# Tap loads three apart, even phases turned first, a longer warm-up: one change to the start of a tuned convolution-and-joint kernel

## The chip, the cores and the metric

The kernel runs on one core of a Trainium2 chip. The metric is the device time of one execution in microseconds (us), the median of several. A second number that this text uses a lot is the span of the profiled execution; the time is 1.8 us longer than the span.

## The reference, cut to what matters

```python
B, T, D, K, U = 2, 4000, 512, 5, 8
xp = pad(x)                                  # x: (B, T, D) in bf16
h = sum(xp[:, i:i+T] @ w1[i] for i in 0..4)  # five taps; w1 is (5, 512, 512)
h = gelu(h)[:, ::2]
f = sum(hp[:, i:i+T1] @ w2[i] for i in 0..4)
f = gelu(f)[:, ::2]
j = tanh((f @ w_f)[:, :, None] + (g @ w_g)[:, None])
out = j @ w_o                                # (2, 1000, 8, 512)
```

## The kernel before

Time steps are kept as four phases (row 4n, 4n+1, 4n+2, 4n+3), with channels on the partitions. The convolution is computed from seven products ("a0", "b1", "b3", "a3", "b2", "a1", "a2") of sums and differences of phases, except for one piece: in the first tile, output column blocks 0 and 1 are computed tap by tap ("direct"), because that needs no sums of taps and can start as soon as one tap is there. "xf" makes a sum or difference on VectorE, "shift" a copy by one column on ScalarE. A small planner derives all waits between engines from the buffers that each operation reads and writes; loads are all issued by SyncE, in program order.

The first 256 columns of each phase of x come raw (`xr`, two loads of 512 KB) and are turned by TensorE; the rest comes by transposing DMAs (`load_x`).

```python
NWARM = 8
# ... cut
memset(zero[:])                                   # on GpSimd
# ... cut
act(warm[0:1], warm[1:2], ACT.Gelu_apprx_tanh)
xr_in = [load_xr(rt) for rt in range(2)]

def load_w1(i, after=None):
    o = load_w("sp", w1_sb[i], w1[i].rearrange("(k c) d -> c k d", c=P))
    if after is not None:
        o.deps[("dma", after.idx)] = True         # SyncE waits until that load has landed

load_w1(0)
for i in (1, 3, 4, 2):
    load_w1(i, xr_in[1])
for ph in (2, 3, 1, 0):
    load_x(0, ph, 272, 528)                       # transposing loads, second part of tile 0/1
# ... cut: load_x for two more segments

warm_mm(NWARM)
for rt in range(2):                               # half of the rows
    for pp in range(2):                           # even phases (0), odd phases (1)
        # ... cut: eight transposes on TensorE into bank 4 + 2 * pp + rt
        # even: copy to xs[0] on VectorE; odd: copy on ScalarE
    warm_mm(1 + rt)
# ... cut
for w in ("a0", "b1", "a3"):
    t0.shift(w)
for w in ("a1", "a2", "b3", "a0", "b1", "a3"):
    t0.xf(w)
wsum13(w1_sb, w1_t, "dve")
w1sums(1, "s")
for i in (0, 1, 3):
    direct(i)                                     # 16 matmuls of 254 columns each
filt("a0", "b1")                                  # a0 uses tap 0's weights, b1 tap 1's
direct(4)
filt("b3", "a3")
direct(2)
# ... cut
for w in ("a0", "b1", "a3"):
    t1.shift(w)                                   # ScalarE: wait for transposing loads
# ... cut: VectorE's sums
filt("b2", "a1", "a2")
for m in (0, 1):
    t0.gelu(m, ps.pair(m * NT, 256, NA))          # ScalarE: frees banks 0 and 1 for tile 1
```

## Time and profile before

| | before |
|---|---|
| time, median of the first 3 executions (lowest to highest) | 280.64 us (280.13 to 281.23) |
| span of the profiled execution | 278.82 us |
| first and second raw x load landed | 4.03, 5.28 us |
| taps 0, 1, 3, 4, 2 landed | 7.62, 10.74, 12.41, 13.81, 15.31 us |
| the four transposing loads of tile 1 landed | 16.16, 18.55, 19.30, 21.02 us |
| tap 0's matmuls start | 8.31 us |
| tile 1's first matmul (246 columns) | 23.81 us |

The landing times are those of the last of the sixteen marks that each load leaves on its semaphore in the trace. The Trainium skill, "DMA: Bandwidth & Descriptors", section "Why a DMA increments its semaphore by 16 and not by 1", says that a load is split over up to sixteen DMA engines which finish independently, and that only the full sixteen mean that all has landed.

The page of before, span, busy times, and the chain that ended last:

```profile
span 278.8 us, 3866 instructions
...
PE 273.8 (98%) x1435; PEld 138.8 (50%) x1435; DVE 188.1 (67%) x243; ACT 163.2 (59%) x193; POOL 30.9 (11%) x39
...
PE 95%; DMA 3%; issue 0%; DVE 0%; SPq 0%; DVEq 0%
```

The same chain in order of time (start, length, what it was):

```profile
1.17 4.11 DMA xr_64<-in_x_dram
...
5.30 5.44 DMA w_sb<-in_w_dram
...
10.78 264.00 PE acc L298 x1368
```

From 10.78 us TensorE works without a pause for 264 us. Nothing that the change touches lies inside that stretch but its first 13 us, so the change can win at the two ends only. The stretch begins when a tap load lands.

TensorE's timeline at the start (start, length, engine, line, operation, operands, count; in brackets the idle time before and what ended it):

```profile
4.68 1.91 PE L365 MATMUL acc<-ident,xr_63 128*128 128x128 bf16 x16
...
6.82 1.11 PE L365 MATMUL acc<-ident,xr_64 128*128 128x128 bf16 x16
...
8.31 1.90 PE L298 MATMUL acc<-xs_49,w_sb 128*128 128x254 bf16 x16
10.78 3.65 PE L298 MATMUL acc<-xs_49,w_sb 128*128 128x254 bf16 x32 [0.57 <-DMA w_sb<-in_w_dram]
...
23.81 0.37 PE L298 MATMUL acc<-xt_54,w_sb 128*128 128x246 bf16 x2
```

The two groups of sixteen transposes are the turning; the second, at a faster clock, takes 1.11 us where the first took 1.91. Tap 0's sixteen matmuls begin at 8.31, and the next ones wait for tap 1. The last line is tile 1's first matmul; its place measures how far ahead or behind TensorE is once the start is over.

ScalarE just before that, the copy "a3" of tile 1 and the two GELUs of tile 0:

```profile
21.04 1.02 ACT L291 ACTIVATE xt_54<-xs_49 128x984 bf16<-128x984 bf16 x1 [1.44 <-DMA xs_49<-in_x_dram]
21.97 1.06 ACT L291 ACTIVATE hT_61<-acc 128x508 bf16<-128x508 f32 x2
```

The copy waits for the fourth transposing load (landed 21.02); the GELUs stand behind it. They read the banks that tile 1's first matmuls write.

And the end, VectorE's last casts and SyncE's last two issues:

```profile
275.42 0.75 DVE L704 CAST ost_85<-acc 128x256 bf16<-128x256 f32 x2
...
275.90 0.93 SPq L712 DMA_DIRECT2D out_dram<-ost_85  x2
```

### The profile page before, as it was taken

How to read it: one execution, taken by the hardware profiler on the slowest of the kernel's cores; microseconds unless marked ns; L12 is line 12 of the kernel's file. 1: busy time of each engine (PE TensorE's matmuls, PEld its weight loads, DVE VectorE, ACT ScalarE, POOL GpSimd, SP SyncE). 2: the span in 40 equal slices, each digit the busy share in tenths (PEclk: the TensorE clock that was granted, in tenths of full speed). 3: DMA queues.
4: the chain of work that ended last, by engine and by line, in shares of the span. 5: the costliest groups of instructions: out<-in, count | busy, mean ns of one | idle time of the engine just before them, and what ended most of it. 6: DMA issues, size and time to landing. Idle time of an engine off the chain costs nothing.

```text
span 278.8 us, 3866 instructions
## 1 busy us (share of the span) xinstructions
PE 273.8 (98%) x1435; PEld 138.8 (50%) x1435; DVE 188.1 (67%) x243; ACT 163.2 (59%) x193; POOL 30.9 (11%) x39
## 2 busy tenths in 40 slices
PE   8999999999999999999999999999999999999995
PEld 4799954444444444444444444444444444444442
DVE  0899979866997676685434364776665766766764
ACT  2659738338327633822346475948957957966930
POOL 1000000079995000000000000000000000000000
PEclk9999999999999999999999999999999999999999
DMA  6999999992000000000000020444444445444444
GB/s 232 308 158 228 206 207 172 286 314 84 0 0 0 2 0 0 0 2 0 0 2 0 1 75 21 151 151 153 153 153 160 149 145 168 144 153 155 145 150 139
DMA packets 54719, 31.85 MB, mean 114 GB/s; under 512 B 31646, under 2 KB 54446, under 8 KB 54702
## 3 DMA queue, kind: packets, MB, share of 16 engines
q1 hardware_dynamic: 54702, 31.62, 42.4%
q8 instruction: 11, 0.18, 0.3%
q14 instruction: 6, 0.05, 0.1%
HBM read 7.86 MB, written 16.38 MB: 87 GB/s over the span
## 4 chain that ended last, share of the span: by engine, by line
PE 95%; DMA 3%; issue 0%; DVE 0%; SPq 0%; DVEq 0%
PE acc L298 95%; DMA w_sb<-in_w_dram 2%; DMA xr_64<-in_x_dram 1%; DVE ost_85 L704 0%; SPq L321 0%; DVEq L238 0%; DVE ost_84 L704 0%
## 5 line engine op out<-in xcount | busy, mean ns | idle before, releaser
L298 PE MATMUL acc<-wo_sb,jT 128*128 128x512 bf16 (+1 forms) x504 | 108.3, 377 | 0.0
L298 PEld LDWEIGHTS acc<-wo_sb,jT 128*128 128x128 bf16 x504 | 49.3, 98 | 58.8
L298 PE MATMUL acc<-xt_55,w_sb 128*128 128x500 bf16 (+1 forms) x192 | 42.1, 357 | 0.0
L291 ACT ACTIVATE jT<-feT_79,geT 128x1000 bf16<-128x1000 f32 (+6 forms) x44 | 35.8, 889 | 0.0
L291 ACT ACTIVATE jT<-feT_78,geT 128x1000 bf16<-128x1000 f32 (+4 forms) x40 | 35.1, 948 | 0.0
L298 PE MATMUL acc<-xt_54,w_sb 128*128 128x500 bf16 (+1 forms) x160 | 33.2, 342 | 0.0
L298 PEld LDWEIGHTS acc<-xt_55,w_sb 128*128 128x128 bf16 x192 | 18.8, 98 | 18.2
L291 ACT ACTIVATE cs_65<-acc 128x500 f32<-128x500 f32 (+2 forms) x13 | 7.0, 539 | 32.2 <-PE acc L298 32.2
L298 PEld LDWEIGHTS acc<-xt_54,w_sb 128*128 128x128 bf16 x160 | 15.6, 98 | 13.1
L291 ACT ACTIVATE cs_66<-acc 128x500 f32<-128x500 f32 (+2 forms) x13 | 7.0, 537 | 22.5 <-PE acc L298 22.5
L298 PE MATMUL acc<-xs_49,w_sb 128*128 128x254 bf16 (+2 forms) x112 | 15.7, 286 | 0.6 <-DMA w_sb<-in_w_dram 0.6
L291 ACT ACTIVATE ost_92<-acc 128x512 bf16<-128x512 f32 x10 | 6.0, 597 | 16.4 <-PE acc L298 16.4
L704 DVE CAST ost_81<-acc 128x512 bf16<-128x512 f32 x11 | 7.6, 691 | 10.4 <-PE acc L298 10.4
L704 DVE CAST ost_87<-acc 128x512 bf16<-128x512 f32 x10 | 6.9, 692 | 10.3 <-PE acc L298 10.3
L298 PE MATMUL acc<-xs_49,w_t 128*128 128x246 bf16 (+2 forms) x72 | 13.8, 315 | 0.0
L287 DVE TENSOR_TENSOR ty_68<-ty_68,acc 128x1000 f32<-128x1000 f32 (+2 forms) x9 | 9.7, 1077 | 5.2 <-PE acc L298 5.2
L287 DVE TENSOR_TENSOR ty_67<-ty_67,acc 128x1000 f32<-128x1000 f32 (+2 forms) x9 | 9.7, 1077 | 5.1 <-PE acc L298 5.1
L298 PEld LDWEIGHTS acc<-xs_49,w_sb 128*128 128x128 bf16 x112 | 10.7, 97 | 4.1 <-DMA w_sb<-in_w_dram 0.8
L291 ACT ACTIVATE ost_86<-acc 128x512 bf16<-128x512 f32 x10 | 5.9, 593 | 11.4 <-PE acc L298 11.4
L287 DVE TENSOR_TENSOR ty_69<-ty_69,acc 128x1000 f32<-128x1000 f32 (+1 forms) x8 | 8.5, 1061 | 3.5 <-PE acc L298 3.3
L298 PE MATMUL acc<-xt_55,w_t 128*128 128x500 bf16 (+1 forms) x48 | 10.0, 340 | 0.0
L704 DVE CAST ost_85<-acc 128x512 bf16<-128x512 f32 (+1 forms) x12 | 7.7, 646 | 2.6 <-PE acc L298 2.6
(113 smaller groups left out, 368.4 us busy)
## 6 DMA issues: line engine op xcount, KB each, us to landing
w_sb<-in_w_dram SPq DMA_DIRECT2D x10, 512.0 KB, 6.7
out_dram<-ost_81 SPq DMA_DIRECT2D x11, 128.0 KB, 1.9
out_dram<-ost_83 SPq DMA_DIRECT2D x10, 128.0 KB, 1.9
out_dram<-ost_85 SPq DMA_DIRECT2D x10, 128.0 KB, 1.9
out_dram<-ost_89 SPq DMA_DIRECT2D x10, 128.0 KB, 1.9
out_dram<-ost_82 SPq DMA_DIRECT2D x9, 128.0 KB
out_dram<-ost_84 SPq DMA_DIRECT2D x9, 128.0 KB
out_dram<-ost_86 SPq DMA_DIRECT2D x9, 128.0 KB
```

Source lines behind the costliest of these rows:

```text
L287: pl.op(eng, lambda e: e.tensor_tensor(out=o.ap, in0=a.ap, in1=b.ap, op=op), (a, b), (o,))
L291: pl.op("act", lambda e: e.activation(o.ap, i.ap, func, scale=scale, bias=0.0 if bias is None else bias.ap), rd, (o,))
L298: ins = e.matmul(o.ap, lhsT=l.ap, rhs=r.ap, start=start and n == 0, stop=stop and n == len(pairs) - 1, skip_group_check=not check)
L704: pl.op("dve", lambda e, o=o, v=v: e.tensor_copy(out=o.ap, in_=v.ap), (v,), (o,))
```

## The change

The intent: let tap 1 be on its way earlier, so that TensorE does not wait for it; start tap 0 earlier, by turning the even phases (all it needs) first; put one product of tap 0's weights right behind tap 0, as work that needs no further load; keep TensorE's clock up by a longer unbroken warm-up that starts sooner; and split the last output row's two halves over two engines.

```diff
-    NWARM = 8
+    NWARM = 10
-        memset(zero[:])
+        zv = zero[:]
+        pl.op("dve", lambda e: e.memset(zv.ap, 0.0), (), (zv,))
...
+        came = [load_xr(rt) for rt in range(2)]
         act(warm[0:1], warm[1:2], ACT.Gelu_apprx_tanh)
-        xr_in = [load_xr(rt) for rt in range(2)]
...
-        load_w1(0)
+            return o
+        came.append(load_w1(0))
         for i in (1, 3, 4, 2):
-            load_w1(i, xr_in[1])
+            came.append(load_w1(i, came[-3]))
...
-        for rt in range(2):
-            for pp in range(2):
+        for pp in range(2):
+            for rt in range(2):
...
-            warm_mm(1 + rt)
...
-            if which == "b3" and keep:
+            if which == "a0" and keep:
+                tt("dve", o(0), src[2, :, off - 1:off - 1 + n], ph(2), sub)
+            elif which == "b3" and keep:
...
-        for w in ("a0", "b1", "a3"):
+        for w in ("b1", "a3"):
             t0.shift(w)
-        for w in ("a1", "a2", "b3", "a0", "b1", "a3"):
+        for w in ("a0", "a1", "a2", "b3", "b1", "a3"):
             t0.xf(w)
...
-        for i in (0, 1, 3):
-            direct(i)
-        filt("a0", "b1")
+        direct(0)
+        filt("a0")
+        direct(1)
+        direct(3)
+        filt("b1")
...
-                if jt % 6 == 5 and not last:
+                if h == 1 or jt % 6 == 5 and not last:
...
-                    pl.dma("sp", lambda e, ...
+                    pl.dma(("sp", "act")[h], lambda e, ...
```

More of the change, by code (lines that the diff above doesn't have):

```diff
@@ L711, in bass_standalone__seq2seq_rnn_t_joint__speech_kernel @@
                     dst = out[b, t:t + n, u, cl]
-                    pl.dma("sp", lambda e, src=src, dst=dst: e.dma_start(dst, src.ap), (src,), (), slot_sem[s])
+                    pl.dma(("sp", "act")[h], lambda e, src=src, dst=dst: e.dma_start(dst, src.ap), (src,), (), slot_sem[s])
                     lo += n
```

## The prediction

> **What bounds the kernel.** TensorE. The chain of waits has one unbroken piece of 264.0 us of matmuls, from 10.78 us to 274.78 us of a 278.8 us span, and the mean granted clock is 1.0. Everything the change touches lies before 24 us or after 274 us, so only the two ends can give anything.
>
> **The start, before (timeline and landing times).** The two raw x loads land at 4.03 and 5.28 us, tap 0 at 7.62. Tap 0's sixteen matmuls start at 8.28 (after VectorE's copy of the second half, 7.51 to 8.20), and take about 1.75 us; TensorE then sits 0.57 us until tap 1 lands at 10.74. Taps 1, 3, 4, 2 are all issued from 5.30 on, behind the second x load; only 202 GB/s move between 6 and 7 us, against 350 to 375 GB/s once several loads are queued. On their slowest engine the taps land 1.4 to 1.7 us apart (10.74, 12.41, 13.81, 15.31).
>
> **What the change does.**
> 1. Tap 1 goes out at about 4.05 instead of 5.30 and queues right behind tap 0. Estimate: 7.6 + 1.5 = 9.1 us, then 10.7, 12.2, 13.8. TensorE never waits for a tap again.
> 2. Even phases turned first: tap 0 needs only these. Warm-up: ten matmuls of 427 ns from about 0.95 us (zero is filled by VectorE; before, the first ran at 1.30) end near 5.2. Turns cost 107 ns each cold and 56 ns warm (both seen), the warm clock came at 6.92. Both even copies done near 7.0 to 7.8, tap 0 starts at 7.65 to 8.3. The Trainium skill, "TensorE: Matmul & The Clock Gate", Part 1, says that the window deciding this runs freely, so the instant varies; this trace shows one switch only.
> 3. a0 by one VectorE subtraction from an unaligned operand, no ScalarE copy. Two pages of the skill disagree: "VectorE: DVE Perf Modes", Mode 2x_1P, asks for 4-byte alignment; "Vector Engine (DVE) Microarchitecture Reference", 5.1, says that it makes no difference. Aligned it takes 0.68 us; I expect 0.7 to 1.1. Either way it is ready before tap 0 ends. Its 0.9 us of matmuls bridge the time until tap 1.
>
> Tap 0 then ends at about 9.6 instead of 10.78: 0.8 to 1.4 us gained for TensorE.
>
> **What may take it back.** The transposing x loads are issued after tap 2, which now waits for tap 1: first issue about 9.6 instead of 7.41. Before, the first of them was stuck in its issue for 4.97 us and its packets hung until 15.07, when tap 2 finished on the slowest engine; as tap 2 comes 1.5 us earlier, I expect no delay. It matters: the last of the four (landing 21.02) gates ScalarE's a3 shift (21.04), which stands ahead of the two GELUs (end 23.03) that free the banks of the next tile's first matmul at 23.81. Slack is only about 0.8 us, so I take 0.2 us off. A landing after 22 us would cancel the gain.
>
> **The tail.** The last half row goes to ScalarE and its own DMA issue. Before, its cast started at 275.75 and its issue at 276.38; now about 275.65 and 276.1: 0.25 us.
>
> **Sum.** 280.64 - 1.2 + 0.2 - 0.25 = 279.4 us. Range 278.5 to 280.4. Faster by over 2%: 0.01; within 2%: 0.98; slower: 0.01.
>
> **What would show it.** Tap 1 landed before 9.6; no TensorE idle between tap 0 and the end; next tile's matmuls (first 246-column ones) starting at 22.5 to 23.0; fourth transposing load landed at or before 21; last output issue near 276.1 less the shift; middle unchanged at about 264 us.
>
> **What would make it wrong.** Transposing loads 1.5 us or more later; tap 0 slowed by tap 1 beside it; a late warm clock.

## The result, and the profile after

| | before | after |
|---|---|---|
| time, median of 6 (lowest to highest) | 280.79 us (279.54 to 281.23) | 279.36 us (278.72 to 279.52) |
| span of the profiled execution | 278.82 us | 277.59 us |
| taps 0, 1, 3, 4, 2 landed | 7.62, 10.74, 12.41, 13.81, 15.31 | 7.89, 9.29, 10.64, 12.99, 14.51 |
| transposing loads of tile 1 landed | 16.16, 18.55, 19.30, 21.02 | 17.02, 17.79, 18.89, 20.46 |
| tap 0's matmuls start | 8.31 | 7.93 |
| tile 1's first matmul | 23.81 | 22.70 |

The ratio of after to before is 0.9952, with a 95% interval of 0.9929 to 0.9975. (A ratio is the mean time of one kernel's fast runs over that of the other's of the same rounds, so it is not quite the ratio of the medians.)

The page and the chain of after:

```profile
span 277.6 us, 3862 instructions
...
PE 272.9 (98%) x1434; PEld 138.1 (50%) x1434; DVE 188.0 (68%) x243; ACT 162.7 (59%) x193; POOL 30.5 (11%) x38
...
PE 96%; DMA 2%; SPq 0%; ACT 0%; issue 0%
```

```profile
1.63 6.25 DMA w_sb<-in_w_dram
...
7.93 266.62 PE acc L298 x1392
...
274.57 0.38 ACT ost L291
```

The unbroken stretch of matmuls now begins with tap 0, at 7.93, and no load interrupts it. TensorE's timeline:

```profile
5.41 2.08 PE L367 MATMUL acc<-ident,xr 128*128 128x128 bf16 x32
7.93 1.92 PE L298 MATMUL acc<-xs,w_sb 128*128 128x254 bf16 x16 [0.44 <-DMA w_sb<-in_w_dram]
9.68 1.03 PE L298 MATMUL acc<-xt,w_sb 128*128 128x254 bf16 x8
10.55 3.64 PE L298 MATMUL acc<-xs,w_sb 128*128 128x254 bf16 x32
...
22.70 1.00 PE L298 MATMUL acc<-xt,w_sb 128*128 128x246 bf16 x8
```

All 32 transposes are one group; tap 0 waits for its load; a0's eight matmuls stand behind it; tap 1's follow with no idle time. ScalarE before tile 1, and the end of the kernel:

```profile
20.48 1.02 ACT L291 ACTIVATE xt<-xs 128x984 bf16<-128x984 bf16 x1 [1.50 <-DMA xs<-in_x_dram]
21.41 1.07 ACT L291 ACTIVATE hT<-acc 128x508 bf16<-128x508 f32 x2
```

```profile
273.70 1.02 DVE L709 CAST ost<-acc 128x512 bf16<-128x512 f32 x2 [0.17 <-PE acc L298]
274.57 0.38 ACT L291 ACTIVATE ost<-acc 128x256 bf16<-128x256 f32 x1 [3.73 <-PE acc L298]
274.99 0.38 ACTq L717 DMA_DIRECT2D out_dram<-ost  x1
```

The account of this pair of executions closes: tile 1 starts 23.81 - 22.70 = 1.11 us earlier. Of these, 0.73 us are the wait for tap 1 (from tap 0's first matmul to tile 1 it took 15.50 us before, 14.77 after) and 0.38 us are tap 0's earlier start (8.31 to 7.93). From there to the start of the last matmul both take 251.56 us (275.37 - 23.81 and 274.26 - 22.70). From the last matmul's start to the end of the span it is 3.45 us before and 3.33 after, 0.12 us less. 1.11 + 0.12 = 1.23 us, which is the difference of the spans (278.82 - 277.59).

That is an account of one execution of each. The experiments ask whether it holds for others.

### The profile page after: what moved, and what is told of

Same layout as the page of the kernel before. It is cut to its first block, busy times and chain, and to the rows that moved or that the text cites. A ratio compares the mean times of both kernels' runs of the same rounds, so it can differ in the third digit from the quotient of the medians.

```text
span 277.6 us, 3862 instructions
## 1 busy us (share of the span) xinstructions
PE 272.9 (98%) x1434; PEld 138.1 (50%) x1434; DVE 188.0 (68%) x243; ACT 162.7 (59%) x193; POOL 30.5 (11%) x38
## 3 DMA queue, kind: packets, MB, share of 16 engines
HBM read 7.86 MB, written 16.38 MB: 87 GB/s over the span
## 4 chain that ended last, share of the span: by engine, by line
PE 96%; DMA 2%; SPq 0%; ACT 0%; issue 0%
PE acc L298 96%; DMA w_sb<-in_w_dram 2%; SPq L322 0%; ACT ost L291 0%
## 5 line engine op out<-in xcount | busy, mean ns | idle before, releaser
L709 DVE CAST ost<-acc 128x512 bf16<-128x512 f32 (+1 forms) x105 | 72.2, 689 | 35.6 <-PE acc L298 35.6
L298 PE MATMUL acc<-xt,w_sb 128*128 128x500 bf16 (+2 forms) x352 | 75.3, 350 | 0.0
L291 ACT ACTIVATE jT<-feT,geT 128x1000 bf16<-128x1000 f32 (+5 forms) x84 | 70.9, 918 | 0.0
L298 PEld LDWEIGHTS acc<-xt,w_sb 128*128 128x128 bf16 x352 | 34.4, 98 | 31.3
L520 DVE SCALAR_TENSOR_TENSOR ty<-acc,cs 128x500 f32<-128x500 f32 (+2 forms) x52 | 29.7, 613 | 23.8 <-PE acc L298 22.9
L287 DVE TENSOR_TENSOR ty<-ty,acc 128x1000 f32<-128x1000 f32 (+2 forms) x26 | 27.9, 1072 | 14.4 <-PE acc L298 13.6
L298 PE MATMUL acc<-xs,w_t 128*128 128x500 bf16 (+2 forms) x136 | 29.9, 342 | 0.0
L298 PE MATMUL acc<-xs,w_sb 128*128 128x254 bf16 (+2 forms) x144 | 23.8, 305 | 0.4 <-DMA w_sb<-in_w_dram 0.4
L291 ACT ACTIVATE xt<-xs 128x2000 bf16<-128x2000 bf16 (+2 forms) x14 | 21.5, 1568 | 3.7 <-DMA xs<-in_x_dram 3.7
L291 ACT ACTIVATE hT<-ty 128x1000 bf16<-128x1000 f32 (+2 forms) x18 | 17.4, 965 | 1.7 <-DVE ty L287 1.6
L298 PE MATMUL acc<-fT,wf_sb 128*128 128x500 bf16 x64 | 13.8, 374 | 0.0
```

The costliest lines, as they stand in the source:

```text
L287: pl.op(eng, lambda e: e.tensor_tensor(out=o.ap, in0=a.ap, in1=b.ap, op=op), (a, b), (o,))
L291: pl.op("act", lambda e: e.activation(o.ap, i.ap, func, scale=scale, bias=0.0 if bias is None else bias.ap), rd, (o,))
L298: ins = e.matmul(o.ap, lhsT=l.ap, rhs=r.ap, start=start and n == 0, stop=stop and n == len(pairs) - 1, skip_group_check=not check)
L520: pl.op("dve", lambda e, o=o, f=f: e.scalar_tensor_tensor(out=o.ap, in0=d.ap, scalar=f, in1=c.ap, op0=ALU.mult, op1=add), (d, c), (o,))
L709: pl.op("dve", lambda e, o=o, v=v: e.tensor_copy(out=o.ap, in_=v.ap), (v,), (o,))
```

## The experiments

The first four kernels (e1 to e4) ran on one chip, the other eight on another; there is no e5. Each has 5 rounds, except e6 and e7 with 3. "Before of the same rounds" is the kernel before, on the same chip.

My first theory (A) was that of the prediction: because tap 1 is issued at 5.30 behind the second x load, it lands near 10.7 in every execution, and TensorE waits. Rival B: it is the earlier start of tap 0 that counts.

### Pacing alone

Before, with only the tap loads' waits changed (run e1_pace):

```diff
-        xr_in = [load_xr(rt) for rt in range(2)]
+        came = [load_xr(rt) for rt in range(2)]
...
-            load_w1(i, xr_in[1])
+            came.append(load_w1(i, came[-3]))
```

> The kernel before with one thing changed: each tap load waits for the load three ahead of it (tap 1 goes out when the first x load has landed). Theory A (the idle time before tap 1 was the cost, and pacing removes it): tap 1 lands near 9.3 us instead of 10.74, tap 0's matmuls still start near 8.3 and end near 10.0, TensorE goes on without idling; the first 246-column matmul starts at 23.1 to 23.3 instead of 23.81; time 0.5 to 0.7 us below before. Rival B (the earlier start of tap 0 by even phases first is what counts): no more than 0.2 us gained.

Measured: tap 1 landed at 9.12, tap 0's matmuls started at 8.30. The timeline of TensorE in this run:

```profile
8.30 4.94 PE L298 MATMUL acc<-xs,w_sb 128*128 128x254 bf16 x44
...
23.05 1.00 PE L298 MATMUL acc<-xt,w_sb 128*128 128x246 bf16 x8
```

One group from tap 0 on: the idle time is gone, as theory A says, and tile 1 starts at 23.05, 0.76 us before the place in the profile of before. But the times say less: ratio 0.9989 (0.9974 to 1.0003), 0.3 us instead of 0.5 to 0.7, and not clear of noise. Before was itself faster in these rounds (median 279.67) than in the first comparison (280.79). Something in before varies.

### Everything but pacing and tail

After, with the old waits of the tap loads and the old tail (run e2_even):

```diff
-            came.append(load_w1(i, came[-3]))
+            came.append(load_w1(i, came[1]))
...
-                if h == 1 or jt % 6 == 5 and not last:
+                if jt % 6 == 5 and not last:
...
-                    pl.dma(("sp", "act")[h], lambda e, ...
+                    pl.dma("sp", lambda e, ...
```

> The kernel after with the old pacing (taps 1, 3, 4, 2 all wait for the second x load) and the old tail; even phases first, longer warm-up, a0 used behind tap 0 are kept. Theory A says that tap 1 still lands near 10.7, but tap 0 (about 7.8 to 9.6) and now also a0's 0.86 us of matmuls are done by then, so TensorE idles only from about 10.5 to 10.75: first 246-column matmul at 22.9 to 23.1, time 0.6 to 0.9 us below before. So pacing and bridging are two cures of one wait and do not add up. Rival B (pacing is needed for any gain): no more than 0.2 us below before.

Measured: tap 1 landed at 9.54, not near 10.7, although it was again issued behind the second x load. Tap 0 ran from 7.39, a0 from 9.14, tap 1 from 10.01, without idle time; tile 1 at 22.15. Ratio 0.9984 (0.9964 to 1.0005). The bridge worked as said: without a0's matmuls TensorE would have stood from 9.1 to 9.6. The landing contradicts theory A.

### After without the bridge

Run e3_nobridge:

```diff
-        direct(0)
-        filt("a0")
-        direct(1)
-        direct(3)
-        filt("b1")
+        for i in (0, 1, 3):
+            direct(i)
+        filt("a0", "b1")
```

> The kernel after with a0's matmuls put back behind taps 0, 1, 3. In the profile of after tap 1 had landed at 9.29, before tap 0's matmuls ended near 9.7, so theory A expects no difference to after beyond 0.2 us: first 246-column matmul at 22.6 to 22.9, time 1.0 to 1.4 us below before. Rival (the bridge is what covers the wait even with pacing): TensorE idles 0.3 us or more before tap 1's matmuls and the time is 0.3 us or more above after's.

Measured: tap 1 at 8.49; tap 0, 1 and 3 in one group from 7.50 (48 matmuls); tile 1 at 22.25; ratio 0.9984 (0.9969 to 0.9998). No idle time: with pacing, the bridge covers nothing in this execution. Tile 1 came a little earlier than I had said (22.6 to 22.9) because tap 0 started earlier than in the profile of after. The time was 0.4 us below before's, not the expected 1.0 to 1.4.

### Even phases first, without pacing, bridge and tail

The edits of the last two together (run e4_even_nobridge).

> The kernel after with the old pacing, the old tail and a0's matmuls put back behind taps 0, 1, 3: of the start only the even phases first and the longer warm-up remain. Theory A: tap 0's matmuls start at 7.7 to 8.0 but TensorE then idles about 1 us until tap 1 lands near 10.7; first 246-column matmul at 23.7 to 23.9 and time as before within 0.2 us. Rival B: 0.3 to 0.5 us gained, as much as tap 0 starts earlier.

```profile
7.86 5.38 PE L298 MATMUL acc<-xs,w_sb 128*128 128x254 bf16 x48
...
22.61 1.00 PE L298 MATMUL acc<-xt,w_sb 128*128 128x246 bf16 x8
```

Theory A failed: no idle time, since tap 1 landed at 9.33 and tap 0 only ended at 9.6. The ratio, 0.9996 (0.9981 to 1.0010), is "as before within 0.2 us", as theory A had said, but not for its reason. I looked at the sixteen marks of tap 1 again. In the profile of before, fourteen of them stand between 8.64 and 9.13, and two at 10.55 and 10.74. So 10.74 was two stragglers, and that is theory C. (They were not of tap 1 alone: taps 3 and 4 in the same profile also have two marks that come 1.2 us or more after the fourteenth, and tap 2 no longer.)

### Before and after again

The next four texts are those of before_again, after_again, before_third and after_third, which are the two kernels unchanged. A "look" is one profiled execution.

> The kernel before itself, a second look at its start, and a control of the noise: ratio 1.000 within 0.002. The four runs so far showed tap 1 landing at 9.3 to 9.5 us even with the old pacing, which speaks against my theory A. Theory A (with the old pacing tap 1 lands near 10.7 in every execution, because it is issued at 5.3): tap 1 at 10.5 to 10.9 again, and TensorE idle about 0.6 us before its matmuls. New theory C (10.74 was a straggler: fourteen of its sixteen parts were there by 9.13, and such stragglers come in some executions only): tap 1 at 9.1 to 9.6, tap 0's matmuls from 8.1 to 8.3, no idle time behind them, first 246-column matmul at 22.9 to 23.1.

> The kernel after itself beside before on the same chip. Theory A: ratio near 0.995 again. Theory C: what remains for certain is tap 0's earlier start (0.4 to 0.8 us) and the tail (0.14 us), so the ratio is 0.9965 to 0.9985 where before has no straggler, and larger gains come only from executions of before with one; first 246-column matmul at 22.2 to 22.8.

> The kernel before, a third look. Its executions so far fall in two groups, 279.2 to 279.7 and 280.5 to 281.2. Theory C says that the start of the next tile is tap 1's landing plus 13.1 us, so the profiled execution's first 246-column matmul is at 22.4 to 22.7 if its time is 279.2 to 279.6, and at 23.6 to 24.0 with tap 1 landing at 10.5 to 10.9 if its time is above 280.4. If a long execution shows tap 1 on time, theory C is wrong about the long group.

> The kernel after again, beside e8 and e9 on the same chip: ratio to before 0.995 to 0.998, first 246-column matmul at 22.2 to 22.8, no execution above 279.8 us.

TensorE's timeline of the second and of the third look at before:

```profile
7.10 1.90 PE L298 MATMUL acc<-xs,w_sb 128*128 128x254 bf16 x16
9.40 1.81 PE L298 MATMUL acc<-xs,w_sb 128*128 128x254 bf16 x15 [0.40 <-DMA w_sb<-in_w_dram]
```

```profile
7.39 1.90 PE L298 MATMUL acc<-xs,w_sb 128*128 128x254 bf16 x16
9.73 1.48 PE L298 MATMUL acc<-xs,w_sb 128*128 128x254 bf16 x12 [0.44 <-DMA w_sb<-in_w_dram]
```

Tap 1 landed at 9.35 and 9.69: no stragglers, as theory C says. But TensorE still waited for it, which theory C had not said for the second look: tap 0 had started early there, at 7.10 and 7.39 instead of 8.1 to 8.3, because the full clock came at 4.41 and 5.00 us (6.92 in the first). So the wait for tap 1 is in all three looks at before, and its end is tap 1's landing: tile 1 started 13.07 us after it each time (23.81 - 10.74, 22.42 - 9.35, 22.76 - 9.69). Part of what an early clock gives is lost in before to this wait.

The third look's time was 279.56 us, and tile 1 at 22.76 misses the 22.4 to 22.7 that I had put beside such a time by 0.06.

After's second and third look: tap 1 at 8.69 and 8.95, tap 0 from 7.80 and 7.20, tile 1 at 22.56 and 21.96 (the latter earlier than the 22.2 I had as a lower edge), ratios 0.9956 (0.9932 to 0.9980; a larger gain than the 0.9965 to 0.9985 of theory C, in rounds in which before had long executions) and 0.9981 (0.9962 to 1.0000; just outside the 0.995 to 0.998 that I had said). Before against itself gave 0.9978 (0.9952 to 1.0004; I had allowed 0.002) and 1.0016 (0.9993 to 1.0040). So a single ratio here is uncertain by some 0.2%, and the ratios of e1 to e4, 0.9984 to 0.9996, can't rank the parts of the change; only the traces can.

The looks so far in one table. "Full clock" is the instant from which the trace records the whole clock as granted, "first matmul" is tap 0's; the rule beside it is worked out below.

| run | full clock | tap 0 landed | first matmul | tap 1 landed | tile 1 | rule |
|---|---|---|---|---|---|---|
| before | 6.92 | 7.62 | 8.31 | 10.74 | 23.81 | tap 1 + 13.07 |
| before_again | 4.41 | 6.88 | 7.10 | 9.35 | 22.42 | tap 1 + 13.07 |
| before_third | 5.00 | 6.95 | 7.39 | 9.69 | 22.76 | tap 1 + 13.07 |
| e4_even_nobridge | 6.26 | 6.76 | 7.86 | 9.33 | 22.61 | first + 14.75 |
| e2_even | 4.51 | 7.34 | 7.39 | 9.54 | 22.15 | first + 14.76 |
| e1_pace | 6.89 | 7.74 | 8.30 | 9.12 | 23.05 | first + 14.75 |
| e3_nobridge | 5.51 | 7.06 | 7.50 | 8.49 | 22.25 | first + 14.75 |
| after | 5.67 | 7.89 | 7.93 | 9.29 | 22.70 | first + 14.77 |
| after_again | 6.14 | 7.29 | 7.80 | 8.69 | 22.56 | first + 14.76 |
| after_third | 4.62 | 7.15 | 7.20 | 8.95 | 21.96 | first + 14.76 |

Two chains run against each other. Without the bridge, tile 1 starts at the later of "first matmul + 14.76" and "tap 1 + 13.07". In before the second is the later one in three of three looks. Every kernel of the table that has pacing, or the bridge, is on the first rule. The one with neither, e4, is there by the luck of a late clock: its two sides were 22.62 and 22.40. In after's third look the second side would have been 8.95 + 13.07 = 22.02, so that there alone the bridge covered something with pacing, 0.06 us.

The times don't contradict this, but they don't show it either. Of the 51 executions of before in all these comparisons, 37 lie between 279.13 and 280.19 (mean 279.59) and 14 between 280.39 and 281.38 (mean 280.85). With only 0.2 us between them, the two groups are my division. The 42 executions of the kernels with pacing and unchanged transposing loads (after, e1, e3, and two below) have none over 279.84; that highest one is e1's, whose clock came as late (6.89) as in before's first look. The 12 of e2 and e4, without pacing, have three over 279.84. The highest, 280.33, is of e2, where the bridge would have hidden most of a wait for a tap 1 that landed at 10.74 (estimate: less a0's matmuls, 9.68 to 10.55 after, tile 1 is at 10.74 + 13.07 - 0.87 = 22.94, and the time 279.8). So something else can also lengthen an execution. The only profiled execution of before's upper group is the first one (280.62 us), with the two stragglers; I did not catch another. That all long executions have this cause is not shown.

### The transposing loads held back

The prediction named one way to lose the gain. After (run e6_late_x), with

```diff
-            load_x(0, ph, 272, 528)
+            load_x(0, ph, 272, 528).deps[("dma", came[-1].idx)] = True
```

(and `load_x` returning its load), so that the first transposing load waits for tap 2's landing, and the same with the GELUs ahead of the copy (run e7_late_x_gelu):

```diff
-        for w in ("a0", "b1", "a3"):
+        for w in ("a0", "b1"):
             t1.shift(w)
...
+        for m in (0, 1):
+            t0.gelu(m, ps.pair(m * NT, 256, NA))
+        t1.shift("a3")
         for w in ("a1", "a2", "a3"):
             t1.xf(w)
         filt("b2", "a1", "a2")
-        for m in (0, 1):
-            t0.gelu(m, ps.pair(m * NT, 256, NA))
```

> The kernel after, its first transposing x load held until tap 2 has landed (about 14.5 us instead of issuing at 9.7). Tests the prediction's one way to lose the gain: the fourth of these loads gates ScalarE's a3 copy, which stands ahead of the two GELUs that free the next tile's banks. Expected: fourth landing at 22.5 to 25, first 246-column matmul at that landing plus 2.2 us (24.7 to 27), TensorE idle before it by what it is late, time 2 to 4 us above after. Rival (the GELUs and banks have more slack than I read): start below landing plus 1.5 us.

> As e6_late_x, but with the two GELUs put ahead of ScalarE's a3 copy, so that they no longer wait for the fourth transposing load. If the order on ScalarE is the gate, the first 246-column matmul comes back to about 22.7 whatever the landing, and TensorE waits only later, for VectorE's a1 operand of that tile (landing plus 0.9 us or more, first wanted 1.7 us after the tile's start): 1 to 2.5 us of e6's loss come back. If the loads themselves are the gate (operands), nearly nothing comes back.

The timeline of the first, ScalarE and TensorE:

```profile
22.75 1.02 ACT L291 ACTIVATE xt<-xs 128x984 bf16<-128x984 bf16 x1 [1.99 <-DMA xs<-in_x_dram]
23.68 1.07 ACT L291 ACTIVATE hT<-acc 128x508 bf16<-128x508 f32 x2
...
24.32 1.01 PE L298 MATMUL acc<-xt,w_sb 128*128 128x246 bf16 x8 [1.37 <-ACT hT L291]
```

The fourth load landed at 22.73, the copy and the first GELU followed, and TensorE idled 1.37 us until the GELU was done. The gate is real. It is smaller than I had read: tile 1 starts 1.59 us after the landing, not 2.2, because the first matmuls need only the first GELU's bank (the first GELU ended at 24.27, the second at 24.75). The start is 1.54 us later than tap 0's start plus 14.76 would be. The median was 280.31 us (ratio 1.0005, 0.9975 to 1.0035), about 1.2 us above after, less than the 2 to 4 that I had expected.

The second:

```profile
20.14 1.07 ACT L291 ACTIVATE hT<-acc 128x508 bf16<-128x508 f32 x2
22.10 1.02 ACT L291 ACTIVATE xt<-xs 128x984 bf16<-128x984 bf16 x1 [0.89 <-DMA xs<-in_x_dram]
...
22.83 1.00 PE L298 MATMUL acc<-xt,w_sb 128*128 128x246 bf16 x8
```

With the GELUs first, tile 1 starts at 22.83 (first matmul 8.08 + 14.75) although the fourth load landed at 22.07. TensorE then waits only 0.2 us, before the matmuls at 25.56, for VectorE's a3 operand (I had named a1). Median 279.75 us, ratio 0.9978 (0.9945 to 1.0010): 0.6 us of e6's 1.2 came back in the median of four, where I had said 1 to 2.5, and 1.3 us in the profiled pair. So the order on ScalarE was the gate.

In after the gate's slack was 22.70 - (20.46 + 1.59) = 0.65 us. In after's third look it was nought: 20.38 + 1.59 = 21.97, and tile 1 started at 21.96.

### Eight warm-up matmuls, and eight with the GELUs first

Runs e8_warm8 and e9_warm8_gelu:

```diff
-    NWARM = 10
+    NWARM = 8
```

> The kernel after with eight warm-up matmuls instead of ten (that part of the change undone). In the profiles of after the ten end near 5.4 us, while the first x load has been there since 4.0; tap 0's start (7.8 to 7.93) follows the second even copy or tap 0's landing, whichever is later. If the longer warm-up only holds the turning back: turning from 4.55, second even copy done at 7.0 to 7.3, tap 0's matmuls at 7.1 to 7.5 unless tap 0 lands later, first 246-column matmul at 21.8 to 22.3, time 0.2 to 0.5 us below after. Rival (the longer warm-up pays, by an earlier full clock): the clock turns full later than with ten, and the time is after's or 0.2 us above it.

> e8_warm8 with the two GELUs ahead of ScalarE's a3 copy, as in e7_late_x_gelu. With the start pulled forward the gate seen in e6 (fourth transposing load plus 1.6 us) comes near: 20.0 to 20.5 plus 1.6 is 21.6 to 22.1. If it binds in e8, this run starts the next tile 0 to 0.3 us earlier than e8; if it doesn't, it equals e8. A version meant to beat both: ratio to before 0.993 to 0.997.

VectorE and TensorE in the run with eight, then in the run that also has the GELUs first; VectorE's first subtraction (a0) begins when both even copies are done:

```profile
6.90 1.28 DVE L287 TENSOR_TENSOR xt<-xs 128x1016 bf16<-128x1016 bf16 x2
...
8.01 1.15 PE L298 MATMUL acc<-xs,w_sb 128*128 128x254 bf16 x9 [0.98 <-DMA w_sb<-in_w_dram]
```

```profile
7.06 1.29 DVE L287 TENSOR_TENSOR xt<-xs 128x1016 bf16<-128x1016 bf16 x2
...
7.44 1.81 PE L298 MATMUL acc<-xs,w_sb 128*128 128x254 bf16 x15 [0.26 <-DMA w_sb<-in_w_dram]
```

With eight the even phases were ready at 6.90 and 7.06, at full-clock instants of 5.18 and 5.97. With ten they were ready at 7.00, 7.51 and 7.74, at 4.62, 5.67 and 6.14. On a straight line through the values with ten, the two extra matmuls hold the turning back by 0.4 us at a clock of 5.18 and by 0.6 us at 5.97, and the clock came no later with eight. But both profiled executions then waited for tap 0 itself (landed 7.97 and 7.40), so tile 1 started at 22.78 and 22.21, the first of them outside the expected 21.8 to 22.3. The times: medians 278.82 and 278.84, ratios 0.9968 (0.9949 to 0.9986) and 0.9975 (0.9955 to 0.9994), against 279.17 and 0.9981 for after in the same rounds. e9's ratio misses the 0.993 to 0.997 that I had said. Whether eight beats ten is not settled by 0.1% with such intervals; that the longer warm-up pays is not seen anywhere. Between e8 and e9 nothing was seen: in neither did the fourth transposing load bind (20.80 + 1.59 = 22.39 against 22.78, and e9 no longer depends on it).

The same reading, when both even copies are done, can be taken in before. The third looks at before and at after, VectorE's first sum or subtraction:

```profile
7.32 1.28 DVE L287 TENSOR_TENSOR xt<-xs 128x1016 bf16<-128x1016 bf16 x2
```

```profile
7.00 1.28 DVE L287 TENSOR_TENSOR xt<-xs 128x1016 bf16<-128x1016 bf16 x2
```

With the old order (before's three looks and e1) it began at 7.03, 7.32, 8.23 and 8.24, at full-clock instants of 4.41, 5.00, 6.89 and 6.92: a straight line within 0.01 us. Each of the six kernels with even phases first, ten warm-up matmuls and a recorded instant lies 0.13 to 0.14 us below that line, the two with eight 0.5 and 0.7 us below it. So what even phases first gains, the longer warm-up mostly takes back. And the start was then often held up elsewhere: in six of the ten looks with even phases first, after's first and third among them, TensorE idled 0.23 to 0.98 us until tap 0 had landed. The prediction had named tap 0 slowed by tap 1 beside it as a risk. In the nine looks with pacing tap 0 landed at 6.94 to 7.98 (mean 7.49), in the five without at 6.76 to 7.62 (mean 7.11); these overlap, so that pacing delays tap 0 is not shown.

## Why the prediction was right or wrong

The number was right: 279.4 predicted, 279.36 measured. Step by step:

- **Only the two ends can give anything.** Right. From tile 1's start to the last matmul it is 251.56 us in both.
- **The start gains 0.8 to 1.4 us, 1.2 taken.** In the pair of profiled executions it was 1.11. The mechanism, a wait for tap 1 that goes away, is right: it is in three of three looks at before and in none at after. What was wrong is that I took the 10.74 of one execution for the rule, when two of its sixteen parts were late. (The spacing of 1.4 to 1.7 us held: 1.51, 1.51 and 1.57 in the second look.) Without stragglers tap 1 lands at 9.35 to 9.7 in before, and the gain of the start is smaller: from the second and third looks, the mean of tile 1's start is 22.59 before and 22.26 after, 0.33 us (a rough figure, from two looks each at different clock instants). The first comparison's 0.48% rests on six executions of before, four of them in the upper group. Over all executions here the means are 279.93 (51 of before) and 279.12 (18 of after), 0.8 us or 0.3%.
- **Tap 0 starts at 7.65 to 8.3 by even phases first.** It started at 7.93, but mostly by luck. Of the 0.73 us by which the even phases were ready sooner (8.24 to 7.51), 0.6 are the earlier clock (6.92 to 5.67, along the line above) and 0.13 the change; then tap 0's late landing, 7.89, took 0.35 us back. No run shows that the change moves the clock: it came at 4.41 to 6.92 in the four looks with the old start, at 4.51 to 6.26 in the six with ten matmuls.
- **Tap 1 near 9.1, taps after it near 10.7, 12.2, 13.8.** Measured 9.29, 10.64, 12.99, 14.51. The first two are right, the last two landed 0.7 to 0.8 us later than said. Taps 4 and 2 were not waited for.
- **a0's matmuls bridge the time until tap 1.** They stand there, but with pacing there was almost nothing to bridge: in the profile of after tap 1 landed at 9.29 and tap 0's matmuls ended near 9.7, and moving a0 back changed nothing that could be seen (e3). Pacing and bridge are two cures of one wait.
- **The longer warm-up.** I costed it and did not ask what it holds back. Even phases were ready 0.4 and 0.6 us sooner with eight.
- **Alignment of a0.** The prediction left open 0.7 or 1.1 us. It is 0.69, as for an aligned operand (next section).
- **The transposing loads are not delayed, 0.2 us off for the gate.** The first landed 0.86 us later than before and the last 0.56 us earlier. The gate exists (e6, e7), but took nothing: I had counted both GELUs where the first is enough. This term was 0.2 and should have been 0.
- **The tail, 0.25 us.** The last issue came 0.28 us earlier relative to the last matmul (276.38 - 275.37 = 1.01 before, 274.99 - 274.26 = 0.73 after), but its data landed 1.89 us after the issue instead of 1.72, so 0.12 remained. In the looks, six with the old tail have 3.44 to 3.46 us from the last matmul's start to the end, and eight with the new one 3.31 to 3.34. This term was sized at twice its worth.

The two wrong sizes, 0.2 taken off needlessly and 0.13 too much at the tail, and a start of 1.11 for 1.2, nearly cancel: -1.2 + 0.2 - 0.25 = -1.25 against -1.11 - 0.12 = -1.23. The close agreement of the sum is partly luck, as is the 1.11 itself, from one execution of before with a late clock and stragglers and one of after with an earlier clock.

## What to carry to other kernels

When a profile shows an engine waiting for a load, look at how the parts of that load landed, and at a second execution, before taking the landing time for a constant; a gain that was read from one profile with a straggler (1.11 us here) need not be that of the next ones (0.33). Compare starts at the same instant of the full clock, or the clock's luck is taken for the change's gain. Two cures of one wait do not add up. Ask of each instruction that waits for a load what stands behind it on its engine: two GELUs behind a copy were a gate that came into reach as soon as the start moved forward, and moving them ahead took it away at no cost that could be seen (e8 and e9: 278.82 and 278.84 us).

## What the Trainium skill lacked or had wrong

- "VectorE: DVE Perf Modes", section "Mode 2×_1P — pack two bf16 into one 32-bit read", asks for 4-byte alignment. The a0 subtraction has one operand that starts one bf16 element off that grid and took 0.692 us; the aligned sum of the same 128x1016 shape that stood first in before took 0.686. "Vector Engine (DVE) Microarchitecture Reference", section 5.1, says that alignment makes no difference, and is right here. In the profile of after's second look:

```profile
7.74 0.69 DVE L287 TENSOR_TENSOR xt<-xs 128x1016 bf16<-128x1016 bf16 x1
```

- "TensorE: Matmul & The Clock Gate", Part 1, puts the full clock at about 4 us of sustained matmuls, within 0.5 us from run to run, and explains it by a freely running window of about 3.4 us. From the first warm-up matmul to the full clock it was 3.1 us (4.41 - 1.29) to 5.6 us (6.92 - 1.30) in these looks: a wider spread than the sentence says, and at the low end less than one window.
- "DMA: Bandwidth & Descriptors" says that the parts of a load finish independently, and gives no size for it. Here the parts of a 512 KB tap load landed over 0.2 us (tap 2 in before, 15.13 to 15.31) to 2.4 us (tap 3 in before, 10.04 to 12.41); tap 1's in before over 2.1 us (8.64 to 10.74, with fourteen of sixteen done by 9.13). What makes a straggler stays open.
- No page has figures for a last output issue from ScalarE against one from SyncE. Here ScalarE's issue took 0.38 us and the half row landed 1.89 us after its start; SyncE's took 0.45 us and landed after 1.72, but the two halves were then 0.48 us apart, instead of 0.19.
